# The 64-fold copy of the softmax reciprocals on VectorE, and the last three blocks of attention operands rounded two steps apart

## The chip, the cores and the metric

The kernel runs on one core of a Trainium2 chip. Time is device microseconds (us) from the first to the last instruction of that core; the figure quoted for a kernel is the median of its runs. The kernel before took 1139.12 us (three runs, 1136.95 to 1139.88).

The engines are named as the profile names them: PE is TensorE (PEld its weight loads), DVE is VectorE, ACT is ScalarE, POOL is GpSimd, SP is the engine that issues the DMAs.

## The reference, cut to what matters

Three stages follow each other: attention with a learned positional bias, a mixture of experts with a Sinkhorn gate, and a feed-forward layer with ELU. The change is in the attention alone:

```
B, H, S, D = 2, 8, 576, 64
scores = q @ k^T / sqrt(D) + bias            # bias: a small MLP on relative positions
attn = exp(scores - rowmax(scores))
attn = attn / (sum(attn, -1) + 1e-9)         # the reciprocals of this sum
x = attn @ v                                 # 1152 tokens x 512
x = sum_e P[:, e] * (relu(x @ w1[e]) @ w2[e])      # 8 experts, F = 1024
out = elu(x @ w_in) @ w_out
```

All of it is float32. The products that need it are made of three matmuls on operands split into a rounded high part and the rest (`qh`, `ql`, `kh`, `kl` for q and k).

## The kernel before

**Steps.** The attention runs in 40 steps of two heads by up to 128 query rows. A block is a pair of heads of one batch entry; there are eight blocks, four in the first 20 steps and four in the rest, and each is used every fourth step. A step s does the following, and the pieces belong to different steps so that they overlap.

- PE: transposes the exponentials of step s-1 (`tr`, L1313), multiplies step s-2 with v in five pieces (`av`, L1380), transposes the last column block of s-1 together with the copied reciprocals of s-2 (`emit_trl`, L1352), and makes the scores of step s+1 (`sc`, L1258). PE runs these in this order, whatever is ready.
- DVE: for each of the two heads adds the bias to the scores and takes the row maximum (`et,nmx` L1270, letters R and S); between them the reciprocals (L1297, letter Z) and the product of an earlier step with its reciprocals (`xt`, L1414, letter X); then it evacuates the second half of the transposes (L1434, U) and of the late ones (L1360, V). The scores of step s+1 use the same two PSUM tiles as those of step s, so PE may write them only when R and S of step s are done.
- ACT: evacuates the first half of the transposes (L1320, T), copies each reciprocal 64 times (`rb`, L1327, letter K), takes the exponentials (L1285, E and F, whose row sums are read out behind them) and evacuates its part of the late transposes (L1362). After that, in the letter p, it rounds `qh` and `kh` of a later block (L1217), and in the letter g it rounds a piece of the first weights or of the first expert operands (`w1h`, L338; `oh`, L383).
- POOL: adds 1e-9 to the row sums (`rc<-sm`, L1293, letter N), subtracts for `ql` and `kl` (L1221, p), and does the sums and the rest parts of the weights and operands (L319 and L335, L356 and L380, g). Its tensor operations last 0.7 to 1.4 us, the add of 1e-9 0.2 us.

The order within a step is written out by hand as a string of letters: `ORD_S` and `ORD_A` while the bias is being made, `ORD_B` after it (from step 14), `ORD_E` behind the last step. The code emits the letters one after another, and every engine keeps the order in which its instructions were emitted. There is nothing that reorders them later.

**Why the copy exists.** The letter K takes a 128 x 2 tile of reciprocals and writes 128 x 128, each reciprocal 64 times side by side. PE transposes this together with the exponentials, which gives the reciprocals along the free axis, one row of 64 partitions for each head, as the `xt` product needs them.

**Rounding the operands.** `PS` says at which step the rounding of a block is queued (`prep`, lines 1208 and following): two roundings on ACT, then two subtractions on POOL for blocks 4 to 7. Each letter p takes one of these four pieces from the queue. Blocks 4 to 7 are first read by the scores that are emitted in steps 19 to 22. `BG` says at which steps the work of letter g is queued: four jobs of five parts each, one part a step, from step 17 on to step 36.

Everything behind the attention (experts and feed-forward layer, from about 186 us) is ordered by a planner with fixed costs; the attention does not enter into it.

Of the kernel before, what the change touches and what calls it, by code (L numbers as in the profile page):

```python
# [11 lines left out]
ACTF = mybir.ActivationFunctionType  # L12
# [27 lines left out]
BG = [17, 22, 27, 32]  # L40
ACC = [2.6, 3.1]
WARM = 8
PS = [[1, 0], [2, 1], [3, 2], [4, 13], [5, 16], [6, 17], [7, 18]]
ORD_S = "RZMXTSOHUapaMEOHaaNpMFOHaLVQ"
ORD_A = "XRZOTSUapaMEaOHaNpaFLVMHQ"
ORD_B = "RZXTKSNUaaLEaaaFVpppgQ"
ORD_E = "XZKfTNVUaafaaa"
TOFF = [0, 128, 256, 384, 512]
TROW = [128, 128, 128, 128, 64]
# [185 lines left out]
def attention_moe_elu_ffn_kernel(  # L235
# [14 lines left out]
    act, dve, pe, pool, sp = nc.scalar, nc.vector, nc.tensor, nc.gpsimd, nc.sync  # L250
# [906 lines left out]
    def attention(fill):  # L1157
# [24 lines left out]
        rcs = {}  # L1182
        rbs = {}
# [14 lines left out]
        def load_v(i):  # L1198
            hp, b = blocks[i]
            vt = vpool.tile([128, 5, 128], F32, tag="v", name="vt")  # L1200
            sp.dma_start(out=vt, in_=vp[b, hp])
            vts[blocks[i]] = vt
# [121 lines left out]
        def emit_spread(s):  # L1324
            r = TROW[steps[s][2]]
            rbs[s] = rbp.tile([128, 128], F32, tag="rb", name="rb")
            act.activation(  # L1327
                out=rbs[s][0:r].rearrange("p (h d) -> p h d", h=2),
                in_=rcs.pop(s)[0:r].unsqueeze(2).to_broadcast([r, 2, 64]),
                func=ACTF.Copy,  # L1330
            )

        def emit_trl(s):
# [92 lines left out]
        def run_step(s):  # L1426
            d = s - LAG
            cur, tr = s < NS, 0 <= d < NS
            for x in ORD_S if s < 3 else ORD_A if no[0] < GRP else ORD_B if cur else ORD_E:
                if x == "T" and tr:  # L1430
# [10 lines left out]
                elif x in "EF" and cur:  # L1441
                    emit_exp(s, "EF".index(x))
                elif x == "N":
                    if 1 <= s <= NS:
                        emit_norm(s - 1)
                elif x == "Z":
                    if 2 <= s:
                        emit_recip(s - 2)
                elif x == "K":
                    if s - 2 < NS:  # L1450
                        emit_spread(s - 2)
                elif x == "X":
                    x_evac()
                elif x == "a":
                    av(1)
                elif x == "M":
                    bias_p()
                elif x == "O":
                    bias_o()
                elif x == "H":  # L1460
                    bias_hh()
                elif x == "p":
                    for _ in range(3 if s < 4 else 1):
                        prep_next()
                elif x == "g":
                    do_bg(1)
                elif x == "L":
                    bias_loads(s)
                elif x == "f":
                    fill_pe(s)  # L1470
# [139 lines left out]
        for s in range(NS + LAG):  # L1610
# [7 lines left out]
            if s in LV:  # L1618
                load_v(LV.index(s))
            for i, s0 in PS:  # L1620
                if s == s0:
# [15 lines left out]
            if s == 15:  # L1637
                w = csb[:, C_WG:C_WG + 4 * E].rearrange("p (k e) -> p k e", k=4)
                dve.memset(wg32, 0.0)
                dve.tensor_copy(wg32[:, :, 0:E], w)  # L1640
        emit_recip(NS - 1)
        emit_spread(NS - 1)
        aT[NS] = atp.tile([128, 10, 128], F32, tag="aT", name="aT")
        while av_q:
# [81 lines left out]
```

## Time and profile before

| | |
|---|---|
| runs | 1139.12 us median, 1136.95 to 1139.88 |
| profiled execution | 1136.95 us, of which the span of the instructions is 1135.2 us |
| busy, share of the span | PE 98%, PEld 86%, DVE 78%, ACT 55%, POOL 7% |
| chain that ended last | PE 89%, ACT 4%, DVE 3%, issue 1%, POOL 1% |
| granted PE clock | 0.995 over the span, 0.95 up to 97 us, 1.00 after it |

| stretch, us | length | PE | DVE | ACT | POOL busy |
|---|---|---|---|---|---|
| 97 to 108 (steps up to 16) | 11.0 | 10.4 | 8.2 | 9.5 | 3.5 |
| 108 to 126 (steps 17 to 21) | 18.0 | 16.5 | 13.0 | 17.6 | 15.9 |
| 126 to 170 (steps 22 to 36) | 44.0 | 44.0 | 37.8 | 42.2 | 26.7 |
| 170 to 186 (last steps) | 16.0 | 15.4 | 11.1 | 11.3 | 0.7 |
| 186 to 1135.2 (rest) | 949.2 | 942.1 | 735.1 | 453.4 | 21.2 |

Busy time counts each instruction's record, and records of one engine overlap by up to 0.1 us, so a busy share near 1 need not mean that the engine has no free time. What a step costs is read from the distance between equal instructions of two steps.

### The profile page before, as it was taken

How to read it: one execution, taken by the hardware profiler on the slowest of the kernel's cores; microseconds unless marked ns; L12 is line 12 of the kernel's file. 1: busy time of each engine (PE TensorE's matmuls, PEld its weight loads, DVE VectorE, ACT ScalarE, POOL GpSimd, SP SyncE). 2: the span in 40 equal slices, each digit the busy share in tenths (PEclk: the TensorE clock that was granted, in tenths of full speed). 3: DMA queues.
4: the chain of work that ended last, by engine and by line, in shares of the span. 5: the costliest groups of instructions: out<-in, count | busy, mean ns of one | idle time of the engine just before them, and what ended most of it. 6: DMA issues, size and time to landing. Idle time of an engine off the chain costs nothing.

```text
span 1135.2 us, 20836 instructions
## 1 busy us (share of the span) xinstructions
PE 1111.3 (98%) x8062; PEld 975.9 (86%) x8062; DVE 884.1 (78%) x1896; ACT 619.5 (55%) x1426; POOL 74.3 (7%) x106
## 2 busy tenths in 40 slices
PE   7799999999999999999999999999999999999998
PEld 3467898999998989999898998989899887999896
DVE  7798787768877888878888788787665579888876
ACT  7999997543344444434444343434334366866663
POOL 0002750000000000000000000000000013000000
PEclk8999999999999999999999999999999999999999
DMA  6667530301232232332323323231111100021002
GB/s 207 206 214 256 170 87 20 112 19 38 93 103 94 93 112 70 107 103 83 112 88 100 108 68 113 95 109 52 51 57 38 56 20 19 21 73 38 22 17 83
DMA packets 36034, 100.14 MB, mean 88 GB/s; under 512 B 3808, under 2 KB 3936, under 8 KB 35936
## 3 DMA queue, kind: packets, MB, share of 16 engines
q1 hardware_dynamic: 35936, 98.82, 26.5%
q8 instruction: 63, 1.03, 0.4%
q14 instruction: 35, 0.29, 0.1%
HBM read 77.16 MB, written 21.64 MB: 87 GB/s over the span
## 4 chain that ended last, share of the span: by engine, by line
PE 89%; ACT 4%; DVE 3%; issue 1%; POOL 1%; ACTq 0%; DVEq 0%; POOLq 0%
PE y L751 42%; PE m L558 39%; PE av L1380 2%; PE sc L1258 2%; PE tr L1313 1%; ACT et L1285 1%; ACT ht L1505 1%; PE bps L1523 1%; ACT o L1555 1%; DVE et L1270 0%; PE av L1352 0%; POOL kl L1221 0%; DVE c L662 0%; DVE o L1557 0%; ACT aT L1320 0%
## 5 line engine op out<-in xcount | busy, mean ns | idle before, releaser
L558 PE MATMUL m<-oh,w1h 128*128 128x256 f32 (+1 forms) x1120 | 330.5, 295 | 0.9 <-ACT p L571 0.5
L558 PE MATMUL m<-ol,w1h 128*128 128x256 f32 (+1 forms) x1120 | 329.3, 294 | 0.1
L558 PE MATMUL m<-oh,w1l 128*128 128x256 f32 (+1 forms) x1120 | 329.0, 294 | 0.0
L751 PE MATMUL y<-w2h,hh 128*128 128x512 f32 x720 | 281.6, 391 | 0.7 <-ACT hh L665 0.6
L751 PE MATMUL y<-w2l,hh 128*128 128x512 f32 x720 | 281.5, 391 | 0.8 <-DVE w2l L457 0.8
L751 PE MATMUL y<-w2h,hl 128*128 128x512 f32 x720 | 281.6, 391 | 0.0
L558 PEld LDWEIGHTS m<-oh,w1h 128*128 128x128 f32 x1120 | 210.2, 188 | 7.5 <-ACT u L571 1.1
L558 PEld LDWEIGHTS m<-ol,w1h 128*128 128x128 f32 x1120 | 210.1, 188 | 5.6 <-DVE ol L457 0.5
L558 PEld LDWEIGHTS m<-oh,w1l 128*128 128x128 f32 x1120 | 210.4, 188 | 0.0
L571 ACT ACTIVATE u<-m 128x256 f32<-128x256 f32 (+1 forms) x160 | 65.5, 409 | 197.0 <-PE m L558 196.8
L751 PEld LDWEIGHTS y<-w2h,hl 128*128 128x128 f32 x720 | 135.2, 188 | 27.9 <-DVE hl L668 0.4
L751 PEld LDWEIGHTS y<-w2h,hh 128*128 128x128 f32 x720 | 135.2, 188 | 26.0 <-ACT hh L665 0.9
L751 PEld LDWEIGHTS y<-w2l,hh 128*128 128x128 f32 x720 | 135.2, 188 | 25.3 <-DVE w2l L457 1.1
L782 DVE SCALAR_TENSOR_TENSOR acc<-y,P,acc 128x512 f32<-128x512 f32 x126 | 94.6, 750 | 59.6 <-PE y L751 59.5
L621 ACT ACTIVATE hh<-c 128x512 fp32r<-128x512 f32 (+3 forms) x128 | 68.9, 558 | 60.4 <-DVE c L590 60.4
L624 DVE SCALAR_TENSOR_TENSOR hl<-c,hh 128x512 fp32r<-128x512 f32 (+3 forms) x128 | 77.6, 607 | 24.9 <-ACT hh L621 22.1
L571 ACT ACTIVATE p<-m 128x256 f32<-128x256 f32 (+1 forms) x160 | 65.6, 410 | 54.5 <-PE m L558 51.4
L1270 DVE CUSTOM_DVE_ANT_0 et<-sc,bt 128x576 f32<-128x576 f32 (+1 forms) x80 | 59.8, 749 | 16.7 <-PE sc L1258 14.7
L450 ACT ACTIVATE w2h<-raw 128x512 fp32r<-128x512 f32 x80 | 48.5, 627 | 40.8 <-PE y L751 40.1
L1285 ACT ACTIVATE et<-et,nmx 128x576 f32<-128x576 f32 (+1 forms) x80 | 61.6, 773 | 0.7 <-DVE nmx L1270 0.7
L457 DVE TENSOR_TENSOR w2l<-raw,w2h 128x512 fp32r<-128x512 f32 x80 | 53.9, 691 | 9.1 <-ACT w2h L450 9.1
L590 DVE TENSOR_TENSOR c<-u,p 128x256 f32<-128x256 f32 (+1 forms) x80 | 37.3, 466 | 24.6 <-ACT u L571 24.1
(147 smaller groups left out, 1496.2 us busy)
## 6 DMA issues: line engine op xcount, KB each, us to landing
raw<-w1p SPq DMA_DIRECT2D x32, 512.0 KB, 3.4
raw<-w2p SPq DMA_DIRECT2D x32, 512.0 KB, 3.2
scr<-o SPq DMA_DIRECT2D x36, 295.5 KB, 2.5
bt<-scr SPq DMA_DIRECT2D x16, 576.0 KB, 4.5
cw<-w1d SPq DMA_DIRECT2D x16, 512.0 KB, 4.0
wsc<-ca SPq DMA_DIRECT2D x32, 256.0 KB, 3.5
cw<-w2d SPq DMA_DIRECT2D x16, 512.0 KB, 4.0
raw<-wsc SPq DMA_DIRECT2D x16, 512.0 KB, 3.6
```

The source lines that it names most:

```text
L450: act.activation(out=dst(bh.get()), in_=src(), func=ACTF.Copy)
L457: lambda e: eng[e].tensor_tensor(out=dst(bl.get()), in0=src(), in1=dst(bh.get().bitcast(F32)), op=ALU.subtract),
L558: lambda e, w=w, o=o, j=j, k=k: pe.matmul(x["ap"](bank), w.get()[:, ai, j, :], o.get()[:, bi, j, :], start=(k == 0 and i in (1, 2, 5)), st ...
L571: lambda e: act.activation(out=b.get()[:, 0:N], in_=x["ap"](bank), func=ACTF.Copy),
L590: lambda e: eng[e].tensor_tensor(out=blk(b.get()[:, half * N:half * N + N], rev), in0=ap(p), in1=ap(q), op=ALU.add),
L621: op([("A", cA(w))], lambda e: act.activation(out=hh(), in_=ap(), func=ACTF.Relu), r=sk, w=wh, after=gate_)
L624: lambda e: dve.scalar_tensor_tensor(out=bl.get()[:, d], in0=ap(), scalar=0.0, in1=hhf(), op0=ALU.max, op1=ALU.subtract),
L751: lambda e, a=a, w=w, f=f, i=i, y=y, c=c: pe.matmul(y.get(), a.get()[:, c], w.get(), start=(f == 0 and i == 0), stop=(f == 3 and i == 2)),
L782: lambda e: dve.scalar_tensor_tensor(out=a.get(), in0=y.get(), scalar=P[0][:, n, e_:e_ + 1], in1=a.get(), op0=ALU.mult, op1=ALU.add),
L1258: pe.matmul(sc[h][0:r, x, 0:HALF], q[d, qc], k[d, kc], start=i == 0, stop=i == 2, tile_position=(64 * h, 0))
L1270: dve.tensor_tensor_reduce(out=e.rearrange("p (x j) -> p x j", x=2), in0=sc[0:r, :, 0:HALF], in1=biast[hp, t][0:r, h].rearrange("p (x j) - ...
L1285: act.activation(out=e, in_=e, func=ACTF.Exp, scale=-1.0, bias=nmx[0:r, h:h + 1], accum_out=sm[0:r, h:h + 1])
```

## The change

Three things change, all in the attention behind the bias.

- The letter K is emitted as a copy on DVE (`dve.tensor_copy`) where it was an activation on ACT. The operands and the result are the same.
- In `ORD_B` the letter K moves from behind T to ahead of X. On DVE it so stands right behind the reciprocals Z and ahead of the product X and of the second head's scores S.
- `PS` queues block 6 at step 18 (17 before) and block 7 at step 20 (18 before), and `ORD_B` has two letters p a step where it had three.

```
-PS = [[1, 0], [2, 1], [3, 2], [4, 13], [5, 16], [6, 17], [7, 18]]
+PS = [[1, 0], [2, 1], [3, 2], [4, 13], [5, 16], [6, 18], [7, 20]]
-ORD_B = "RZXTKSNUaaLEaaaFVpppgQ"
+ORD_B = "RZKXTSNUaaLEaaaFVppgQ"
         def emit_spread(s):
             r = TROW[steps[s][2]]
             rbs[s] = rbp.tile([128, 128], F32, tag="rb", name="rb")
-            act.activation(
-                out=rbs[s][0:r].rearrange("p (h d) -> p h d", h=2),
-                in_=rcs.pop(s)[0:r].unsqueeze(2).to_broadcast([r, 2, 64]),
-                func=ACTF.Copy,
+            dve.tensor_copy(
+                rbs[s][0:r].rearrange("p (h d) -> p h d", h=2), rcs.pop(s)[0:r].unsqueeze(2).to_broadcast([r, 2, 64])
             )
```

All 28 copies move, 24 of 128 partitions and 4 of 64. The order of PE and of SP is the same in both kernels; below `emit_spread` the line numbers of the changed kernel are two lower.

DVE, one step with the bias done. `et,nmx` is R or S with its read-out of the maximum, `rc` the reciprocals, `xt` the product, `aT` the two evacuations. Before:

```order
L1270 ISA et,nmx<-sc,bt 128x576
L1270 ISA nmx 128x1
L1297 RECIPROCAL rc<-rc 128x2
L1414 TENSOR_TENSOR xt_105<-av,aT 128x128
L1270 ISA et,nmx<-sc,bt 128x576
L1270 ISA nmx 128x1
L1434 COPY aT<-tr 128x8x64
L1360 COPY aT<-av 128x2x64
```

and now:

```order
L1270 ISA et,nmx<-sc,bt 128x576
L1270 ISA nmx 128x1
L1297 RECIPROCAL rc<-rc 128x2
L1327 COPY rb<-rc 128x128
L1412 TENSOR_TENSOR xt_105<-av,aT 128x128
L1270 ISA et,nmx<-sc,bt 128x576
L1270 ISA nmx 128x1
L1432 COPY aT<-tr 128x8x64
L1358 COPY aT<-av 128x2x64
```

One instruction is added to each step, between the reciprocals and the product; the second head's scores stand behind it.

POOL, from step 17 on, where the last three blocks are rounded. `ql` and `kl` are the subtractions of a block, `st` the sums and `w1l` the rest parts of the first weights, `rc` the add of 1e-9 that opens each step. Before:

```order
L1221 TENSOR_TENSOR ql<-ring,qh 128x576
L1293 TENSOR_SCALAR rc<-sm 128x2
L1221 TENSOR_TENSOR kl<-ring,kh 128x576
L319 TENSOR_TENSOR st<-raw 128x256
L319 TENSOR_TENSOR st<-st,raw 128x256
L319 TENSOR_TENSOR st<-raw 128x256
L319 TENSOR_TENSOR st<-raw,st 128x256
L1293 TENSOR_SCALAR rc<-sm 128x2
L1221 TENSOR_TENSOR ql<-ring,qh 128x576
L1221 TENSOR_TENSOR kl<-ring,kh 128x576
L335 TENSOR_TENSOR w1l<-raw,w1h 128x512
L1293 TENSOR_SCALAR rc<-sm 128x2
```

and now:

```order
L1221 TENSOR_TENSOR ql<-ring,qh 128x576
L1221 TENSOR_TENSOR kl<-ring,kh 128x576
L319 TENSOR_TENSOR st<-raw 128x256
L319 TENSOR_TENSOR st<-st,raw 128x256
L319 TENSOR_TENSOR st<-raw 128x256
L319 TENSOR_TENSOR st<-raw,st 128x256
L1293 TENSOR_SCALAR rc<-sm 128x2
L335 TENSOR_TENSOR w1l<-raw,w1h 128x512
L1293 TENSOR_SCALAR rc<-sm 128x2
L1221 TENSOR_TENSOR ql<-ring,qh 128x576
L1221 TENSOR_TENSOR kl<-ring,kh 128x576
L335 TENSOR_TENSOR w1l<-raw,w1h 128x256
```

The subtractions of blocks 6 and 7 now stand two steps apart, one add of 1e-9 stands between those of block 6 and the piece of weights of the step before, and none stands between `ql` and `kl` any more. On ACT the roundings `qh` and `kh` of blocks 5, 6 and 7 stand in steps 16, 18 and 20, both of a block together; before they stood in steps 16, 17 and 18/19.

## Rows read from the trace of the kernel before

**Rows 1.** Timeline of PE: start us, duration us, engine, line, operation, names, shapes, count.

```profile
107.26 0.38 PE L1258 MATMUL sc<-kh,qh 64*128 64x288 f32 x2
...
130.79 0.38 PE L1258 MATMUL sc<-kh,qh 64*128 64x288 f32 x2
```

**Rows 2.** Timeline, all engines, one step; brackets: idle time before, what ended it.

```profile
152.09 0.73 PE L1313 MATMUL tr<-csb,et 64*128 64x64 f32 x16
...
152.29 0.76 DVE L1270 CUSTOM_DVE_ANT_0 et<-sc,bt 128x576 f32<-128x576 f32 x1 [0.43 <-PE sc L1258]
152.36 0.63 ACT L383 ACTIVATE oh<-st 128x512 fp32r<-128x512 f32 x1
...
152.91 0.60 ACT L1320 ACTIVATE aT<-tr 128x512 f32<-128x512 f32 x1
...
153.06 0.27 DVE L1414 TENSOR_TENSOR xt<-av,aT 128x128 f32<-128x128 f32 x1
153.07 1.28 POOL L380 TENSOR_TENSOR ol<-st,oh 128x512 fp32r<-128x512 f32 x1 [0.47 <-ACT oh L383]
153.24 0.75 DVE L1270 CUSTOM_DVE_ANT_0 et<-sc,bt 128x576 f32<-128x576 f32 x1
153.40 0.30 ACT L1327 ACTIVATE rb<-rc 128x128 f32<-128x128 f32 x1
153.60 0.77 ACT L1285 ACTIVATE et<-et,nmx 128x576 f32<-128x576 f32 x1
153.91 0.08 DVE L1270 DVE_READ_ACCUMULATOR2_ANT nmx<- 128x1 f32 x1
...
154.36 0.77 ACT L1285 ACTIVATE et<-et,nmx 128x576 f32<-128x576 f32 x1
...
155.01 0.73 PE L1313 MATMUL tr<-csb,et 64*128 64x64 f32 x16
```

**Rows 3.** Timeline, DVE and PE, a step in which PE waited for DVE.

```profile
124.92 0.08 DVE L1270 DVE_READ_ACCUMULATOR2_ANT nmx<- 128x1 f32 x1
...
125.83 0.77 PE L1313 MATMUL tr<-csb,et 64*128 64x64 f32 x16
```

**Rows 4.** Timeline of ACT and DVE where the last blocks are rounded.

```profile
111.91 0.68 ACT L1217 ACTIVATE qh<-ring 128x576 fp32r<-128x576 f32 x1
112.48 0.68 ACT L1217 ACTIVATE kh<-ring 128x576 fp32r<-128x576 f32 x1
113.06 0.63 ACT L338 ACTIVATE w1h<-raw 128x512 fp32r<-128x512 f32 x1
...
120.07 0.17 DVE L1297 RECIPROCAL rc<-rc 128x2 f32<-128x2 f32 x1 [0.49 <-POOL rc L1293]
...
123.96 0.17 DVE L1297 RECIPROCAL rc<-rc 128x2 f32<-128x2 f32 x1 [0.93 <-POOL rc L1293]
```

**Rows 5.** Timeline of POOL and DVE, three places where both read and write SBUF.

```profile
48.50 0.21 POOL L1293 TENSOR_SCALAR rc<-sm 64x2 f32<-64x2 f32 x1 [5.67 <-ACT et L1285]
...
51.91 1.27 DVE L1507 TENSOR_SCALAR ht<-U,csb 128x336 f32<-128x336 f32 x4
52.72 0.54 POOL L1293 TENSOR_SCALAR rc<-sm 128x2 f32<-128x2 f32 x1 [4.01 <-ACT et L1285]
...
937.33 0.75 POOL L356 TENSOR_TENSOR st<-xt,st 128x256 f32<-128x256 f32 x1
937.52 0.84 DVE L651 TENSOR_SCALAR a<-c 128x512 f32<-128x512 f32 x1
...
945.83 0.43 DVE L651 TENSOR_SCALAR a<-c 128x512 f32<-128x512 f32 x1
...
950.94 0.74 POOL L668 TENSOR_TENSOR hl<-c,hh 128x256 fp32r<-128x256 f32 x1 [8.51 <-ACT hh L665]
951.01 0.96 DVE L356 TENSOR_TENSOR st<-xt 128x256 f32<-128x256 f32 x1
```

**Rows 6.** Timeline of PE behind the last step.

```profile
179.01 0.27 PE L1352 MATMUL trl<-csb,rb 64*128 64x64 f32 x1 [0.32 <-ACT rb L1327]
```

## The prediction

> **What bounds the kernel now.** I read the timeline of PE first, to learn what a step of the attention costs. In an undisturbed step PE goes from one group of transposes to the next in 155.01 - 152.09 = 2.92 us [rows 2], without a gap that the timeline names; PE is the bound there. Seven steps lie between the two score groups at 107.26 and 130.79 and take 130.79 - 107.26 = 23.53 us, where seven undisturbed ones take 20.44. So 3.1 us are lost in the stretch in which the last three blocks are rounded [rows 1, 2]. The timelines of the other engines then say why: ACT puts two roundings of 0.57 us and a piece of weights behind each other without a pause, and twice DVE's reciprocals wait for POOL's add of 1e-9, 0.49 and 0.93 us, because POOL is still at its subtractions [rows 4].
>
> Next is how much room DVE has in an undisturbed step, since that is where the new copy goes. In one step PE waited for the second head's maximum; that ended at 125.00 and the next transposes began at 125.83, 0.83 us later [rows 3]. In the undisturbed step it ended at 153.99 and the transposes began at 155.01, 1.02 us later [rows 2]. So the second head's scores may end 0.19 us later before PE notices. Whatever DVE does between the scores of the first head and the end of the second beyond that is paid by PE in full, and by every step behind it.
>
> **The change, part by part.**
>
> *Roundings spread, and ACT without the copy.* ACT's regular work in an undisturbed step is 2.92 less the 0.55 that one piece (`oh`, 152.36 to 152.91) takes, as the transposes come in just then: 2.37 us, of which the copy is 0.20 (153.40 to 153.60) [rows 2]. Without it 0.75 us a step are free. Into the five steps 16 to 20 fall six roundings of 0.57 (111.91 to 112.48, [rows 4]), three pieces of 0.55 and one of half the size, an estimate of 0.3: 5.35 us against 5 x 0.75 = 3.75. So 1.6 us remain of the 3.1, and the 1.4 us of waiting for POOL go with it, as the adds now come between shorter rows of subtractions: **-1.5 us**. What is late next is ACT, in steps 18 and 20, which get both roundings of a block beside a piece of weights. If ACT got no relief at all the term would be 0, and at most it is -3.1.
>
> *Behind the last step* PE waits 0.32 us for a copy that ACT makes late [rows 6]; DVE would make it right behind the reciprocals: **-0.3 us**.
>
> *The copy on DVE, by itself.* No row shows this copy on DVE. Its bounds are zero and the slot of the product `xt`, which has the same 128 x 128 but reads two operands: 153.24 - 153.06 = 0.18 us [rows 2]. I take 0.15. That is under the 0.19 of room, so by itself it costs nothing; with two thirds more it would cost some 0.05 us a step over about 20 steps, 1 us.
>
> *The copy against POOL.* This is the term that decides. Unlike everything else that DVE does in these steps, which reads PSUM or two columns, the copy reads 128 columns from SBUF and writes SBUF, and POOL does the same all the time. What happens elsewhere in this kernel when both do so can be seen [rows 5]. POOL's add on two columns takes 0.21 us alone and 0.54 when DVE runs `ht<-U` (SBUF to SBUF, one operand). DVE's `a<-c` (the same kind) takes 0.43 us alone; begun 0.19 us behind a POOL subtraction of 0.75 it took 0.84, and ended at 938.36, 0.28 us behind the POOL instruction's end at 938.08. And a DVE subtraction begun only 0.07 us behind POOL's took 0.96 us, ending 0.29 us behind POOL's end. So the later of the two stands still until the other has finished.
>
> [...]
>
> Now the place. The copy's turn on DVE comes where `xt` begins now, 0.77 us behind the start of R 152.29 and 153.06, [rows 2]. POOL's long subtraction `ol` began at 153.07, 0.71 us behind the start of ACT's piece `oh` at 152.36. Today that is a tie that nobody feels. But ACT loses 0.20 us of copy ahead of the exponentials, so the second exponential begins at 154.16 instead of 154.36, or a little behind the second head's maximum, which with a copy of 0.15 ends at 154.14; I take 154.20. Everything behind it on ACT, and POOL's subtraction, comes 0.16 us earlier. So POOL starts about 0.15 us ahead of the copy, and the copy waits for 1.28 - 0.15 = 1.13 us. X and the second head's scores wait behind it on DVE, and PE's next scores wait for those: 1.13 + 0.15 - 0.19 = 1.1 us a step. In the next step the same order returns, because ACT's last exponential, and with it POOL, then hangs on the same late maximum. Six steps between 134 and 169 us have such a long subtraction by itself behind ACT's piece (one of them is the one at 153.07): 6 x 1.1 = **+6.6 us**. If the copy came first in them, the term would be 0.
>
> In seven more of these steps POOL begins with sums of 256 columns (0.75 us, [rows 5]) or has the short piece. The wait then lies between 0 and 0.7; I take 0.25 in five of them and 0.5 in two: 5 x 0.2 + 2 x 0.45 = **+1.9 us**. In steps 17 to 23, where POOL is hardly idle, one to four copies may meet a subtraction of 1.4 us, but part of this hides behind ACT, which is late anyway: bounds 0 and +4, I take **+0.8 us**.
>
> *Sum:* -1.5 - 0.3 + 6.6 + 1.9 + 0.8 = +7.5 us. The profiled execution took 1136.95 us (span 1135.2), so 1144.45 by its own time. It was the fastest of three; the median is 2.17 us above it, so on that footing 1146.6. Behind the attention PE is 99% busy and its order does not change, so the shift goes through to the end.
>
> **The rivals.**
>
> [...]
>
> *The copy gets there first.* The 0.15 us by which POOL leads is small. If the copy wins in the six steps, POOL waits 0.1 us for it, which nobody feels; then -1.5 - 0.3 + 1.9 + 0.8 = +0.9 us, 1140.0. It decides at a shift of about 0.15 us between ACT's pieces and the scores. For it: half of ACT's gain is given back if the maximum comes later than I think. Against it: the row at 951.01, where 0.07 us was enough.
>
> *The whole loss goes.* If neither ACT nor POOL is late any more, -3.1 - 0.3 = -3.4 us, 1135.7. Against it stands ACT's 5.35 us in 3.75.
>
> **How the numbers follow.** A measurement of this kernel can tell about 0.3% from no change, 3.4 us. I give the forecast 0.57, the copy first 0.20, the free port 0.18 and the whole gain 0.05. The forecast's own range is 1142 to 1150 (three of the six long waits missing below, the bound of steps 17 to 23 above). With the two rivals next to it, 1136 to 1150 leaves out little. Slower by over 0.3% is the forecast alone, 0.57; faster by as much the last rival, 0.05; the rest, 0.38, is within it.
>
> **What would show it.** DVE's `rb` copies, 0.2 us alone, with durations up to 1.4 us in the steps around 135, 138, 150, 153, 165 and 168 us, ending just behind a POOL subtraction; PE waiting there for DVE's maximum; steps of about 4 us instead of 2.92. The score groups of steps 18 to 24 less far apart than 23.5 us if the copies do not collide there. The prediction is wrong if all `rb` records have one length, or if the undisturbed steps keep their 2.92 us.

## The result and the profile after

The changed kernel takes 1148.84 us (median of 6 runs, 1145.97 to 1149.89); the kernel before took 1139.06 in the same comparison (6 runs, 1135.72 to 1140.06). The ratio is 1.0089 with a 95% interval of 1.0071 to 1.0107, so the kernel is slower by 0.9%, some 9.8 us. The prediction was 1146.6 us, within 1136 to 1150, and slower as the likeliest case. The profiled execution took 1149.61 us with a span of 1147.8. That is 12.6 us more than the span of before: the profiled run of before was 2.1 us quicker than its median, that of after 0.8 us slower than its own.

The new copy is easily found, as it has a line to itself. First its group (busy us, mean ns, idle time ahead), then its summary by line (shortest, median and longest duration in ns, first and last start):

```profile
L1327 DVE COPY rb<-rc 128x128 f32<-128x128 f32 (+1 forms) x28 | 18.2, 650 | 1.0
...
L1327 DVE COPY rb<-rc x28: 218/356/1427, 99.8 to 192.8; 128x128 f32<-128x128 f32 x24, 64x128 f32<-64x128 f32 x4
```

A mean of 650 ns over a median of 356 and a shortest of 218 says that a few copies are very long. Idle time isn't counted here, because DVE shows as busy while the copy stands still. So the view of waits blames the instructions behind it. Of the window 95 to 195 us (us in all, times, longest):

```profile
ACT et L1285 <- DVE nmx L1270: 10.4, 18, 1.0
...
PE av L1350 <- DVE xt L1412: 6.4, 12, 0.8
...
PEld sc L1258 <- DVE nmx L1270: 3.7, 12, 0.4
...
PE m L558 <- DVE nmx L1270: 0.5, 1, 0.5
```

Before, the list of the same window had none of these but 0.6 us of the third, and for the fourth a weight load that waited 0.3 us. PE's list now names `xt`, which is innocent: it stands behind `rb` on DVE. The timeline of one step shows it (DVE, POOL and PE, the step that answers to [rows 2]):

```profile
140.25 0.76 DVE L1270 CUSTOM_DVE_ANT_0 et<-sc,bt 128x576 f32<-128x576 f32 x1 [0.23 <-PE sc L1258]
...
140.90 1.28 POOL L335 TENSOR_TENSOR w1l<-st,w1h 128x512 fp32r<-128x512 f32 x1 [0.47 <-ACT w1h L338]
...
140.94 0.16 DVE L1297 RECIPROCAL rc<-rc 128x2 f32<-128x2 f32 x1
141.13 1.12 DVE L1327 COPY rb<-rc 128x128 f32<-128x128 f32 x1
141.37 0.77 ACT L1285 ACTIVATE et<-et,nmx 128x576 f32<-128x576 f32 x1
...
142.18 0.28 DVE L1412 TENSOR_TENSOR xt<-av,aT 128x128 f32<-128x128 f32 x1
142.38 0.74 DVE L1270 CUSTOM_DVE_ANT_0 et<-sc,bt 128x576 f32<-128x576 f32 x1
...
142.60 0.28 PE L1350 MATMUL av<-csb,et 64*128 64x64 f32 x2 [0.53 <-DVE xt L1412]
...
143.16 0.78 ACT L1285 ACTIVATE et<-et,nmx 128x576 f32<-128x576 f32 x1 [0.94 <-DVE nmx L1270]
```

POOL begins its subtraction 0.23 us ahead of the copy and ends at 142.18; the copy ends at 142.25. The next step's copy begins at 145.04, so this step is 3.91 us long, where [rows 2] had 2.92. Six steps are like that (copies at 141.13, 145.04, 158.08, 161.98, 175.03 and 178.86, all of 1.11 to 1.19 us). A step in which POOL isn't in the way, from the same timeline:

```profile
134.80 0.16 DVE L1297 RECIPROCAL rc<-rc 128x2 f32<-128x2 f32 x1
134.99 0.23 DVE L1327 COPY rb<-rc 128x128 f32<-128x128 f32 x1
135.13 0.28 DVE L1412 TENSOR_TENSOR xt<-av,aT 128x128 f32<-128x128 f32 x1
```

Here `xt` begins 0.33 us behind the start of the reciprocals (at 135.13). Before, in the step of [rows 2], it began 0.08 behind it, at 153.06:

```profile
152.98 0.16 DVE L1297 RECIPROCAL rc<-rc 128x2 f32<-128x2 f32 x1
```

The copy itself takes a slot of 0.14 (134.99 to 135.13). It begins 0.19 behind the reciprocals' start, 0.11 later than `xt` did; it reads their result, and `xt` doesn't. These steps are 134.99 to 137.99, 3.00 us.

Two places in the timeline of PE answer to [rows 1], and behind them stand the last score group and the last transpose:

```profile
110.05 0.63 PE L1258 MATMUL sc<-kh,qh 64*128 64x288 f32 x2
...
136.01 0.53 PE L1258 MATMUL sc<-kh,qh 64*128 64x288 f32 x2
...
186.38 0.81 PE L1258 MATMUL sc<-kh,qh 64*64 64x288 f32 x2
...
195.99 0.27 PE L1350 MATMUL trl<-csb,rb 64*128 64x64 f32 x1
```

The last two of these in the kernel before:

```profile
173.98 0.32 PE L1258 MATMUL sc<-kh,qh 64*64 64x288 f32 x1
...
183.68 0.27 PE L1352 MATMUL trl<-csb,rb 64*128 64x64 f32 x1
```

So the span can be cut up. The three score groups stood at 107.26, 130.79 and 173.98 before. Up to 107.26 it lost 2.79 us, in the rounding stretch 25.96 - 23.53 = 2.43, in the steps behind it 50.37 - 43.19 = 7.18. These are 12.4 of the 12.6 us; behind 186.38 only 0.2 more is lost.

The first 2.79 us were foreseen by no term. The timeline of POOL, DVE and PE in step 14:

```profile
99.75 1.41 POOL L1221 TENSOR_TENSOR ql<-ring,qh 128x576 fp32r<-128x576 f32 x1
99.82 1.43 DVE L1327 COPY rb<-rc 128x128 f32<-128x128 f32 x1
...
101.50 1.52 PE L1378 MATMUL av<-aT,vt 128*64 128x128 f32 x20 [1.24 <-DVE xt L1412]
```

Block 4's operands, which the change doesn't move, are rounded there, and the first copy runs into them with 0.07 us between the two starts. PE waits 1.24 us. Behind that, in this execution, PE's granted clock reads 0.73, 0.50, 0.50 and 0.56 in the four microseconds from 102 on, and then 1.00 again; the columns are length, PE busy, granted clock, DMA share and GB/s:

```profile
101.00:102.00 1.00, 0.50 (x10) 1.00 0.65 118
102.00:103.00 1.00, 1.00 (x18) 0.73 0.96 265
103.00:104.00 1.00, 1.00 (x12) 0.50 1.04 405
104.00:105.00 1.00, 1.00 (x16) 0.50 1.04 417
105.00:106.00 1.00, 1.00 (x20) 0.56 0.57 221
106.00:107.00 1.00, 1.00 (x20) 1.00 0.00 0
```

Before, these microseconds had PE busy throughout and a granted clock of 1.00.

### The profile page after: what moved, and what is told of

Its sections match the earlier page's. It is cut to its first block, busy times and chain, and to the rows that moved or that the text cites. A ratio compares the mean times of both kernels' runs of the same rounds, so it can differ in the third digit from the quotient of the medians.

```text
span 1147.8 us, 20816 instructions
## 1 busy us (share of the span) xinstructions
PE 1117.5 (97%) x8062; PEld 979.4 (85%) x8062; DVE 901.3 (79%) x1924; ACT 617.0 (54%) x1398; POOL 73.2 (6%) x106
## 4 chain that ended last, share of the span: by engine, by line
PE 87%; DVE 6%; ACT 3%; issue 1%; POOL 0%; ACTq 0%; DVEq 0%; POOLq 0%
PE y L751 42%; PE m L558 38%; PE sc L1258 3%; PE av L1378 2%; DVE et L1270 2%; DVE rb L1327 1%; PE bps L1521 1%; ACT ht L1503 1%; PE tr L1313 1%; ACT et L1285 1%; ACT o L1553 1%; POOL st L356 0%; DVE ol L457 0%; PE av L1350 0%; DVE a L658 0%
```

## The experiments

Each run was compared with the kernel before on the same chip; 1138.29 us in the first four, 1137.55 in the next four, 1137.17 in the last two. Ratios are to that kernel, with 95% intervals; they are estimated from all runs of both kernels and differ by up to 0.0012 from the quotients of the medians. In the strings below, K is the copy, X the product `xt`, p one of the four pieces of a block's rounding.

**The copy alone.** The changed kernel with the old spread:

```diff
-PS = [..., [5, 16], [6, 18], [7, 20]]
-ORD_B = "RZKXTSNUaaLEaaaFVppgQ"
+PS = [..., [5, 16], [6, 17], [7, 18]]
+ORD_B = "RZKXTSNUaaLEaaaFVpppgQ"
```

> The copy is on DVE as in the changed kernel, but blocks 6 and 7 are rounded as before (steps 17 and 18, three letters p). Theory (the copy stands still while a POOL tensor instruction runs): the copies of up to 1.4 us stay, and the rounding stretch loses at least what it loses in the changed kernel, so 1148 to 1152 us. Rival (the new places of the roundings make the loss): the time falls back to 1138 to 1141 us.

Measured: 1148.28 us, 1.0100 (1.0085 to 1.0115). The copy alone loses as much as the whole change; the two intervals (1.0071 to 1.0107 for the change) overlap, so they show no difference. One part of the theory failed: the seven steps of [rows 1] take 25.44 us here, a little less than in the changed kernel (25.96) and not at least as much.

**The spread alone.** The kernel before with the new spread; the copy stays on ScalarE:

```diff
-PS = [..., [5, 16], [6, 17], [7, 18]]
-ORD_B = "RZXTKSNUaaLEaaaFVpppgQ"
+PS = [..., [5, 16], [6, 18], [7, 20]]
+ORD_B = "RZXTKSNUaaLEaaaFVppgQ"
```

> The copy stays on ACT and behind T; only the roundings are spread as in the changed kernel. Theory: no DVE instruction of these steps meets POOL, so the steps behind 126 us keep 2.92 us and the rounding stretch loses less than its 3.1 us: 1137.5 to 1139 us. Rival (the spread makes the loss): over 1142 us.

Measured: 1138.18 us, 0.9996 (0.9984 to 1.0009): no difference. Its score groups that answer to [rows 1] are 23.02 us apart in place of 23.53, so the spread by itself takes back 0.5 of the 3.1 us:

```profile
107.70 0.38 PE L1258 MATMUL sc<-kh,qh 64*128 64x288 f32 x2
...
130.72 0.38 PE L1258 MATMUL sc<-kh,qh 64*128 64x288 f32 x2
```

**The copy behind X.** The changed kernel with one letter moved:

```diff
-ORD_B = "RZKXTSNUaaLEaaaFVppgQ"
+ORD_B = "RZXKTSNUaaLEaaaFVppgQ"
```

> As the changed kernel, with the letter K behind X: the copy no longer waits 0.11 us for the reciprocals just ahead of it, nothing else changes. Theory (waiting for POOL): steps without a collision go from 3.00 to 2.92 us, those with one stay near 3.8 to 3.9, so 1146 to 1149 us. Rival (what costs is the copy's own slot with the wait for the reciprocals, not POOL): 1139 to 1141 us.

Measured: 1145.67 us, 1.0070 (1.0054 to 1.0087). The time is 0.3 us below the range of the theory and far above the rival's. X no longer stands behind the copy, but the second head's scores do, and the waits stay. They are a little shorter than expected: behind 134 us, steps with a copy of over 1 us take 3.64 to 3.72 us, not 3.8 to 3.9.

```profile
L1327 DVE COPY rb<-rc x28: 208/312/1383, 100.2 to 186.7; 128x128 f32<-128x128 f32 x24, 64x128 f32<-64x128 f32 x4
```

**The same place, the copy made by a reduction** over an axis of one element:

```diff
-            dve.tensor_copy(
-                rbs[s][0:r].rearrange("p (h d) -> p h d", h=2), rcs.pop(s)[0:r].unsqueeze(2).to_broadcast([r, 2, 64])
-            )
+            dve.tensor_reduce(
+                rbs[s][0:r].rearrange("p (h d) -> p h d", h=2),
+                rcs.pop(s)[0:r].unsqueeze(2).unsqueeze(3).to_broadcast([r, 2, 64, 1]), AX.X, ALU.add,
+            )
```

> As the kernel with K behind X, but the 64-fold copy is made by a sum over an axis of length one, which reads the same 128 columns from SBUF and writes the same tile. [...] Rival (any DVE instruction of 128 columns from SBUF to SBUF waits for POOL): rb records up to 1.4 us and 1146 us or more.

Measured: 1136.34 us, 0.9988 (0.9979 to 0.9998). The same bytes are read and written at the same place, and no copy waits. First its summary, then the timeline of a step in which POOL started 0.35 us ahead:

```profile
L1327 DVE TENSOR_REDUCE rb<-rc x28: 268/276/279, 101.5 to 181.0; 128x128 f32<-128x128 f32 x24, 64x128 f32<-64x128 f32 x4
...
135.60 1.28 POOL L335 TENSOR_TENSOR w1l<-st,w1h 128x512 fp32r<-128x512 f32 x1 [0.47 <-ACT w1h L338]
...
135.76 0.27 DVE L1413 TENSOR_TENSOR xt<-av,aT 128x128 f32<-128x128 f32 x1
135.95 0.28 DVE L1327 TENSOR_REDUCE rb<-rc 128x128 f32<-128x128 f32 x1
136.15 0.75 DVE L1270 CUSTOM_DVE_ANT_0 et<-sc,bt 128x576 f32<-128x576 f32 x1
```

The rival, with records of up to 1.4 us, is excluded: 28 of 28 reductions last 268 to 279 ns. Of a reduction that doesn't wait I had expected 1137 to 1140 us, and it took 0.7 us less than the lower of these. So the reading of [rows 5], that the later of the two stands still, doesn't hold for every DVE instruction that reads and writes SBUF: it holds for the copy (218 to 1427 ns in the changed kernel) and not for this reduction. What it is in the two instructions that makes the difference, no run here shows.

**An additional copy, from SBUF and from PSUM.** Two runs of the kernel before, each with one more DVE instruction ahead of X whose result nothing reads (the diff is shortened):

```diff
-ORD_B = "RZXTKSNUaaLEaaaFVpppgQ"
+ORD_B = "RZDXTKSNUaaLEaaaFVpppgQ"
+        def emit_dummy(s):      # the second run has the second copy in place of the first
+            dm = dmp.tile([128, 128], F32, tag="dm", name="dm")
+            dve.tensor_copy(dm, U[:, 0:128])
+            dve.tensor_copy(dm[0:TROW[steps[s][2]]], scs[s, 1][0:TROW[steps[s][2]], 0, 0:128])
```

> The kernel before, with one more VectorE instruction in each step of the bias stretch between the row maximum and the evacuation X: a copy of 128 columns from SBUF to SBUF that nothing reads. The copy of the reciprocals stays on ScalarE. Theory (a VectorE copy SBUF to SBUF stands behind whatever SBUF-to-SBUF instruction GpSimd has under way, and X and its matmul stand behind it): the same shape as in the changed kernel, copies of 0.23 us alone and above 1 us beside the long GpSimd subtractions, steps of 3.9 us there; 1138.3 plus 5 to 11 is 1143 to 1149 us. Rival (the copy costs only its slot and the reciprocals' result that it waits for is what made it long): no copy over 0.3 us, 1138 to 1140 us. Rival (the loss came with the reciprocals leaving ScalarE): 1138 us.

> As the run with the additional copy, at the same place, but its 128 columns are read from the scores in PSUM, and again nothing reads what it writes. Theory (what waits for GpSimd is a copy whose source is SBUF as well as its target): no duration over 0.35 us, a slot of about 0.26 us against the 0.19 us of room that VectorE has in a steady step, 28 x 0.07 = +2 at the most: 1138 to 1141 us. Rival (any additional VectorE instruction ahead of X stands behind GpSimd): 1143 to 1149 us, as with the copy from SBUF.

Measured: from SBUF 1146.68 us, 1.0084 (1.0064 to 1.0103), from PSUM 1139.74, 1.0022 (1.0010 to 1.0033). The first is as slow as the changed kernel, though the copy waits for no reciprocals and the real copies are still on ScalarE; that excludes both rivals of the first run. Summary by line of the first, then of the second:

```profile
L1336 DVE COPY dm<-U x26: 198/438/1454, 99.4 to 185.2; 128x128 f32<-128x128 f32 x26
```

```profile
L1336 DVE COPY dm<-sc x26: 262/271/273, 100.0 to 178.7; 128x128 f32<-128x128 f32 x22, 64x128 f32<-64x128 f32 x4
```

A copy from PSUM isn't held once. What it costs is its slot: `xt` begins 0.27 us behind the reciprocals where it began 0.08 behind, and the copies follow each other at 3.01 to 3.02 us (133.65, 136.67) in place of 2.92.

**Block 4 one step earlier**, so that its subtractions miss the first copies:

```diff
-PS = [..., [4, 13], [5, 16], [6, 18], [7, 20]]
+PS = [..., [4, 12], [5, 16], [6, 18], [7, 20]]
```

> The changed kernel with block 4's operands rounded from step 12 on, not 13, and nothing else different. Theory: the copy of step 14 (1.43 us in the changed kernel, under GpSimd's subtraction ql of that block) then starts with GpSimd idle and takes 0.23 us, TensorE doesn't wait 1.24 us for X there, and its granted clock stays at 1.00 between 102 and 106 us: 1.2 us, or 2.7 with the clock, less than the changed kernel's 1148.8, 1146 to 1147.6 us. The collision may move to step 13, where the operands now fall; then it is 1148 to 1149 us. Rival (that one collision is hidden by work that TensorE has queued): 1148.8 us, no difference.

Measured: 1147.34 us, 1.0090 (1.0070 to 1.0110). In the trace what was expected is there: the first three copies take 0.23 us each, the granted clock is 1.00 from 90 to 106 us, and the two score groups around the first are 3.81 us apart in place of 5.33. But PE still waits 0.86 us for X there:

```profile
97.20 0.38 PE L1258 MATMUL sc<-kh,qh 64*128 64x288 f32 x2
...
99.62 1.31 PE L1378 MATMUL av<-aT,vt 128*64 128x128 f32 x20 [0.86 <-DVE xt L1412]
...
101.01 0.38 PE L1258 MATMUL sc<-kh,qh 64*128 64x288 f32 x2
```

That wait costs little: the five steps up to 106.98 take 19.22 us, where the changed kernel's took 21.58 and the kernel before 18.90. So the trace shows 2.4 us regained. The time lies in the range expected, but the ratio is that of the changed kernel, so what the median owes to step 14 stays undecided; an amount up to some 3 us is within the two intervals.

**The reduction with the old spread**, three p pieces in a step as before:

```diff
-PS = [..., [5, 16], [6, 18], [7, 20]]          # the run with the reduction behind X
-ORD_B = "RZXKTSNUaaLEaaaFVppgQ"
+PS = [..., [5, 16], [6, 17], [7, 18]]
+ORD_B = "RZXKTSNUaaLEaaaFVpppgQ"
```

> The copy made by VectorE's reduction over an axis of one element, behind X, as in the run with the reduction, but with blocks 5, 6 and 7 rounded one step apart as before, three p pieces in a step. It tells what the spread adds where the copy doesn't wait. If the gain of that run (1136.3 against 1138.3) comes from the spread: 1137.9 to 1138.5 us. If it comes from ScalarE being rid of the copies: 1136 to 1136.7 us. If it takes both: in between or above.

Measured: 1138.57 us, 1.0006 (0.9993 to 1.0018). Neither the spread alone (0.9996) nor ScalarE's relief alone (1.0006) shows a gain; both together gave 0.9988. The three intervals overlap, so the times alone don't prove that it takes both. The traces say it more clearly: the seven steps of [rows 1], 23.53 us before, take 23.02 with the spread alone, 23.69 with the relief alone and 21.85 with both.

**The changed kernel with nothing but the instruction replaced:** the reduction of above at K's place ahead of X, the new spread.

> The changed kernel with nothing but the instruction of the copy replaced: VectorE makes it as a reduction over an axis of one element, at the copy's own place ahead of X, with the new spread. Theory (all that the copy loses is its waiting for GpSimd, the rest is its slot): the copies' time above 0.23 us adds up to 11.8 us in the trace of the changed kernel and goes; the reduction's slot is 0.05 us longer than an unhindered copy's, 28 x 0.05 = 1.4 at the most: 1148.8 - 11.8 + 1.4 = 1138.4 us, 1.000 of the kernel before, between 0.998 and 1.002. Rival (the place ahead of X costs much by itself, since the copy must wait for the reciprocals there): 1142 us and more, above 1.004.

Measured: 1140.41 us, 1.0020 (1.0008 to 1.0032). This is the cleanest split of the loss: 0.9% with the copy, 0.2% with the reduction in its place. So some 0.7% (7.9 us by the ratios, 6.5 by the medians) is waiting for POOL, and 0.2%, the upper end of what was expected, is the reduction's slot ahead of X; the rival's 1.004 lies outside the interval. That slot is longer than I had put it: 0.40 us from the reciprocals to `xt` in place of 0.08 before and of 0.33 with the copy, and steps of 3.06 us:

```profile
140.76 0.16 DVE L1297 RECIPROCAL rc<-rc 128x2 f32<-128x2 f32 x1
140.96 0.29 DVE L1327 TENSOR_REDUCE rb<-rc 128x128 f32<-128x128 f32 x1
141.15 0.74 POOL L356 TENSOR_TENSOR st<-xt,st 128x256 f32<-128x256 f32 x1
141.16 0.28 DVE L1413 TENSOR_TENSOR xt<-av,aT 128x128 f32<-128x128 f32 x1
...
144.02 0.29 DVE L1327 TENSOR_REDUCE rb<-rc 128x128 f32<-128x128 f32 x1
```

**POOL's long subtractions in halves.** The changed kernel, the copy untouched (the subtraction `ol` of L380 is halved in the same way; that part of the diff is left out):

```diff
-                pool.tensor_tensor(out=lo[:, dst], in0=src, in1=hi.bitcast(F32)[:, dst], op=ALU.subtract)
+                for d, x in halves(dst, src):
+                    pool.tensor_tensor(out=lo[:, d], in0=x, in1=hi.bitcast(F32)[:, d], op=ALU.subtract)
```

> The changed kernel, with GpSimd's subtractions of 512 columns (the lower parts of the operands) issued as two of 256 columns, 0.75 us each in place of one of 1.28. The copy on VectorE is untouched. Theory (the copy stands behind the one GpSimd instruction under way and no longer): beside the long ones it ends after some 0.5 us in place of 1.12, the six steps of 3.9 us become 3.4, and some of the waits of steps 16 to 23 shorten too: 3 to 5 us less than the changed kernel, ratio to before 1.004 to 1.007. Rival (GpSimd's next instruction goes ahead of the waiting copy): the copy waits for both halves, 1.3 us and more, steps of 4.0 us: ratio 1.009 to 1.011. Rival (halves are handed over later by ScalarE's pace, so that the copies go ahead of them): below 1.002.

Measured: 1145.42 us, 1.0067 (1.0052 to 1.0081), as the theory had it. The copy now ends 0.08 us behind the first half:

```profile
141.48 0.73 POOL L339 TENSOR_TENSOR w1l<-st,w1h 128x256 fp32r<-128x256 f32 x1 [0.47 <-ACT w1h L342]
...
141.71 0.58 DVE L1332 COPY rb<-rc 128x128 f32<-128x128 f32 x1
```

POOL's second half begins at 142.17 and takes 0.73 us, 0.69 behind the first; two of POOL's sums of 256 columns that meet no copy are 0.70 apart in the changed kernel (133.62 and 134.32). So the copy doesn't wait for the second half, and the trace doesn't show the second half waiting for the copy either. The six long copies became 0.57 to 0.64 us, and the steps from 141.71 to 145.08 and on to 148.42 are 3.37 and 3.34 us in place of 3.9.

## Why the prediction was right, and where its sum was not

**The copy against POOL in six steps, +6.6.** Right in mechanism, place and size: copies of 1.11 to 1.19 us at just these six steps, 3.90 in place of 2.92 us, 6 x 0.98 = 5.9. The lead of POOL that I had worked out as 0.15 us was 0.23, so the copy stood 0.1 us less. PE meets the delay in two places where I had named one: it waits 0.53 us for `xt`, and then its weight load waits 0.30 for the second head's maximum (143.18). The same feedback keeps it there, as argued: behind a long step ACT's exponential waits for the late maximum (0.94 us at 143.16), and POOL's next subtraction with it. The rival in which the copy comes first is excluded by the rows.

**The copy by itself, 0.** The copy's own slot is 0.14 us, and I took 0.15. But I left out that it reads what the reciprocals have just written, which costs 0.11 more. A slot of 0.25, which is the two thirds more that I had priced at 0.05 us a step, against 0.19 of room is 0.06 us a step; steps without a collision grew by 0.08. The room was read from a step in which PE's weight load waited for that maximum [rows 3]:

```profile
125.05 0.18 PEld L1258 LDWEIGHTS sc<-kh,qh 64*128 64x128 f32 x1 [0.29 <-DVE nmx L1270]
```

Three other slots test it. The reduction behind X takes 0.19 and the steps are 2.94 to 2.95, where 2.92 was due; the reduction ahead of X takes 0.32 and they are 3.06, where 3.05 was due. The additional copy from PSUM takes 0.19 too, but the steps are 3.02, 0.10 more than was due; why isn't shown. In that kernel ACT still makes its own copies.

**Seven more steps, +1.9.** Too high. All the steps behind 136.01 together lost 7.18, of which 5.9 are the six; about 1.3 remain for the others, and that is mostly the slot. The collisions there are three copies of 0.36 us, in steps of 3.14 us.

**The rounding stretch, -1.5 and +0.8.** The -1.5 itself holds: where the copy doesn't wait and ACT has no copy, the same seven steps take 130.89 - 109.04 = 21.85 us in the run with the reduction behind X, 1.7 less than before. The spread alone gave 0.5 and ACT's relief alone nothing, so the 1.7 us come only with both, and not piece by piece, as my sum of ACT's free time had it. And the waits of steps 17 to 23 are not +0.8. Five copies from 112.12 to 127.88 last 1.33, 0.81, 1.38, 1.12 and 1.32 us, and the stretch is 25.96 - 22.07 = 3.9 us longer than with the reduction at the same place, which is the upper bound that I had given (+4). I had let ACT's lateness hide most of it; but in these five steps ACT's second exponential waits 0.17 to 0.93 us for the very maximum that the copy holds up.

**Steps 14 and 15, not in the sum.** I counted collisions from step 17 on, although the copies begin at 99.8 us and block 4's subtractions lie there. It cost 2.7 us in the profiled execution. Of this some 1.5 goes with the lower clock: in the run with the copy alone the same collision (a copy of 1.43 us, PE waiting 1.25) came with a granted clock of 1.00, and the same two steps took 7.87 us, not 9.33. In the run with the halves PE was slow behind it again (the 20 pieces of `av` at 103.25 took 2.40 us, where they took 1.31 in the run with the copy alone), and the two steps took 9.39.

**Behind the last step, -0.3.** PE's wait of 0.32 [rows 6] is gone, but from the last score group to the last transposes it is 9.61 us where it was 9.70. In its place PE waits 0.5 us for DVE's last maximum ahead of its first `m` (189.70), where before only the weight load waited, 0.3 us. The copy's slot is one part of it; how large a part was not tried.

Summed by the trace: 2.8 + 2.4 + 7.2 + 0.2 = 12.6 us between the two spans, where the sum had +7.5. Step 14 (2.7 against nothing) and the rounding stretch (+2.4 against -0.7) were too low by 5.8; the six steps and the seven others were too high by 1.3, and the end of the attention brought +0.2 where I had -0.3. Between the medians the loss is 9.8 us, so the forecast came within 2.2 us of the measured time. That is partly luck: its largest term was right, but two others were not, and the profiled pair of executions lies further apart than the medians. The measured time is 1.2 us below the upper end of the stated range. Two slips of my working change nothing in this: ACT's pieces add up to 5.37 us, not 5.35, and three long waits fewer give 1143.3, not 1142. The free port, to which the chances gave 0.18, was the case that no copy waits for POOL: -1.5 - 0.3 = -1.8 us, 1137.3. No run shows a port; they show that the plain copy waits and that the reduction doesn't, and so a kernel of this kind can be had: the reduction behind X gained 2.0 (1138.29 to 1136.34). It is the one version here that beats the kernel before, by 0.12% with an interval that ends at 0.9998, hardly more than nothing.

## What to carry to other kernels

Before a copy within SBUF is moved to DVE, look at what POOL has under way at that moment. Here DVE was held for the rest of POOL's instruction (a copy of 0.23 us took 1.12 beside a subtraction of 1.28, and 1.43 beside one of 1.41) and everything queued behind the copy with it, while the profile called DVE busy and named the next instruction as the culprit (`xt`, 6.4 us of PE's waiting). Compare the shortest and longest durations of the line to see it (218 and 1427 ns). If the copy must stand there, give it a form that didn't wait here (a reduction over one element, 268 to 289 ns, or a source in PSUM, 262 to 273), put it behind the instruction for which the bottleneck waits (the reduction took 1.0020 ahead of X and 0.9988 behind it), or cut POOL's instructions smaller (1.0067 with the halves, 1.0089 without).

## What the runs showed that was not expected

- A DVE reduction over an axis of one element makes the copy in 268 to 289 ns in two kernels, 56 times, with POOL busy or not (0.28 us at 135.95 and at 105.16 in the run behind X); the plain copy takes 0.21 to 0.23 us alone and up to 1.43.
- The hold ends with the one POOL instruction under way: where that is cut in two, the copy ends 0.08 us behind the first half (copies of 0.57 to 0.64 us in place of 1.11 to 1.19), although the second half has begun by then, 0.69 us behind the first.
- At the same place PE waited 1.24 us in the changed kernel and 1.25 in the one with the halves, and slower matmuls followed (in the first, four microseconds at a granted clock of 0.50 to 0.73; in the second, `av` of 2.40 us in place of 1.31); in the kernel with the copy alone it waited 1.25 too, and the clock stayed at 1.00 (PE busy 0.50, 0.21 and 0.54 in three successive microseconds). What decides it, these runs don't show.
- Reading at once what the instruction ahead has written cost DVE 0.11 us for two columns: the copy of the reciprocals begins 0.19 us behind their start, the copy from PSUM, which doesn't read them, 0.08.
